# Two decode layers on one core: a query slice loaded ahead, output weights multiplied between the last values, smaller down pieces, fewer turning products

## The chip, the core and the metric

One core of a Trainium2 chip runs the whole program. Its engines are TensorE (PE, matrix products), VectorE (DVE), ScalarE (ACT), GpSimd (POOL) and SyncE (SP), whose queue issues nearly all transfers from HBM; 16 DMA engines carry them. The metric is the device time in microseconds (us), lower is better.

## The reference

One token for each of two sequences goes through attention and a gated feed-forward block, twice, with the same weights and the same caches:

```python
# B = 2, D = 576, H = 32 heads of 128, 8192 cached keys and values a head, Df = 4608, all float32
def attention(x):                       # x has been normalised
    q = (x @ wq) as heads
    p = softmax(q . k_cache / sqrt(128))
    return (p . v_cache) as one row @ wo
def feed_forward(x):
    return (gelu_tanh(x @ w_gate) * (x @ w_up)) @ w_down
x = x + attention(layernorm(x)); x = x + feed_forward(layernorm(x))     # layer one
x = x + attention(layernorm(x)); x = x + feed_forward(layernorm(x))     # layer two
```

## The kernel before

**Cache items.** Attention runs over items: 30 *pairs* (two heads of one sequence: 8.4 MB of keys and as much of values) and four *singles* (heads 30 and 31, s0 to s3, half as large). In layer one the singles come last, in the order s0, s1, s2, s3; layer two goes backward, so it begins with s3, s2, s1, s0. The keys and values of s3 and s2, the values of s1 and a quarter of its keys stay in the local memory between the layers and are not loaded again. For each part of an item, DVE multiplies the keys by the query (L490, `multiply`), POOL adds the halves (L494) and DVE reduces them (L500, `add_up`); then follow the maximum (`peak`, DVE L511, a transpose on PE L513, `highest`, DVE L518), the softmax on ACT (L529, L533), its total on PE (L546), the products with the values on PE (`values`, L561) and the joining of the result (`gather`, DVE L571 and L573; `context`, PE L581).

**The area and its queue.** All loads go into one tile, `space`. A class `Space` holds a list of loads in a fixed order; `pump` issues the first one when the place that it wants is clear, and none that stands behind it before. `done(key)` is called where the program has emitted the last use of a load; in the run, the transfer then waits for that use. Between the layers everything goes through a ring of 6,912 columns (`MID` to `END`): first the output weights `wo` of layer one (16 pieces of 1,152 columns, 576 KB: here w0 to w15), then gate and up weights (36 pieces), the down weights (12 pieces of 1,728 columns, 864 KB: d0 to d11), and the query weights of layer two (18 pieces of 1,024 columns, 512 KB: eight of one half, two of the middle rows, eight of the other half). The ring holds 3.5 MB. Scratch for s3 lies in the same ring until s3's scores are done, so only w0 and w1 can be loaded before that.

**Around the change.** In layer one, `values(s3)` is emitted first, then `invert`, `gather`, the products `project` with 14 of the 16 `wo` pieces, `context`, and the last two. In `mlp(0)`, `lower(d0)` stands ahead of `turned(1)` (72 small products that turn the second half of the hidden row, L693) and `gelu(1)`; the other down pieces follow (L715). In layer two, `attention` multiplies the whole first half of the query weights (L416), with `norm` after its first two pieces; ACT copies the queries (L440), `query(0)` (L462) spreads that of s3, and only then can DVE begin; `rest_of_queries` follows on PE behind `query(1)`. The loads behind the query weights are three parts of s1's keys (in the ring), s0's four parts of keys (where s3's keys lay), s0's values (where s3's values lay), and then the pairs: keys into the place of s2's keys and values, values into the place of s1, keys into the place of s0.

At the end, `mlp(1)` turns both halves (72 products each), and multiplies the down weights while their last pieces arrive.

The lines of the queue that the change touches:

```python
sp.at = MID + 2 * PART                                              # the ring's first place
first_down = [(t, lo, lo + 3) for t in range(NT) for lo in (0, 3, 6)]
```

Of the kernel before, what the change touches and what calls it, by code (L numbers as in the profile page):

```python
# [15 lines left out]
P = 128  # L16
# [23 lines left out]
NG = H // GH  # L40

# [54 lines left out]
def decode_layers(ctx, tc, x_in, kc, vc, wq, wo, wg, wu, wd, out):  # L96
# [52 lines left out]

    def middle(key, w, width, where, lo=0, hi=None):  # L150
# [48 lines left out]
    first_down = [(t, lo, lo + 3) for t in range(NT) for lo in (0, 3, 6)]  # L199
# [25 lines left out]
    sp.at = MID + 2 * PART  # L225
# [10 lines left out]
    for t, lo, hi in downs[0]:  # L236
        down(("d", 0, t, lo), mid, t, lo, hi)
    for half in (1, 0):
        for i in range(NW):
            for s in range(2):  # L240
                rows(("wq", 1, half, i, s), wq, HQ, mid, (2 * i + half) * HQ + s * CQ * 2, CQ * 2)
        if half:
            for s in range(2):
                middle(("wq", 1, "m", s), wq, HQ, mid, s * CQ * 2, (s + 1) * CQ * 2)
# [102 lines left out]
    def turn(first=False):  # L347
# [7 lines left out]
        if not first:  # L355
            nc.vector.tensor_copy(wide, x10[:, :, 0:9])
        nc.vector.tensor_copy(x10[:, :, 9:10], x10[:, :, 4:5])
        nc.vector.transpose(xtm, x10.rearrange("p q (r i) -> p i (q r)", i=5)[:, 4, :])
        nc.vector.tensor_mul(
            xm, xtm[:, 0:RW].unsqueeze(1).to_broadcast([P, 5, RW]), mask.unsqueeze(2).to_broadcast([P, 5, RW])  # L360
        )
# [3 lines left out]
        for b in range(B):  # L365
# [3 lines left out]
            )  # L369
        return apart  # L370
# [33 lines left out]
    def attention(layer, items, apart):  # L404
# [3 lines left out]
        def queries(bank, lhs, at, start, stop, s=None):  # L408
            for c in range(4):
# [3 lines left out]
                else:  # L413
                    moving = space[:, at + c * CQ // 2:at + (c + 1) * CQ // 2]
                    to = bank[32 * c:32 * c + WIN, s * CQ // 2:(s + 1) * CQ // 2]
# [13 lines left out]
        else:  # L429
            for i in range(NW):  # L430
                for s in range(2):
                    queries(acc[1], window(1, i), at_of["wq", 1, 1, i, s], i == s == 0, False, s)
                    done(("wq", 1, 1, i, s))
                if i == 0:
                    norm(apart)
            for s in range(2):
                queries(acc[1], only[1], at_of["wq", 1, "m", s], False, s == 1, s)
                queries(xps, only[0], at_of["wq", 1, "m", s], s == 0, False, s)
                done(("wq", 1, "m", s))
            nc.scalar.activation(qsb, acc[1], AF.Copy)  # L440
# [149 lines left out]
        def project(g):  # L590
            n = GH if layer else 2
            for i in range(GH):
# [211 lines left out]
```

## Time and profile before

| | |
|---|---|
| runs | 2707.04, 2707.79, 2709.14 us; median 2707.79 us |
| profiled execution | 2708.16 us, of which the span of its instructions is 2706.1 us and 2.1 us lie around it |
| busy share of the span | DMA queue q1 99.3% of 16 engines; DVE 69%, POOL 43%, PE 35%, ACT 3% |
| read from HBM | 1153.18 MB, 426 GB/s over the span |
| mean granted TensorE clock | 0.627 of full speed |

The page shows one execution in 40 slices with the DMA share and the GB/s of each. A view by windows gives the same for any stretch, with each engine's busy time; the timeline lists instructions with their start and length in us and, in brackets, how long the engine had been idle and what ended it. Records of a fp32 matrix product come in twos, so a piece of 8 products shows as x16.

### The profile page before, as it was taken

How to read it: one execution, taken by the hardware profiler on the slowest of the kernel's cores; microseconds unless marked ns; L12 is line 12 of the kernel's file. 1: busy time of each engine (PE TensorE's matmuls, PEld its weight loads, DVE VectorE, ACT ScalarE, POOL GpSimd, SP SyncE). 2: the span in 40 equal slices, each digit the busy share in tenths (PEclk: the TensorE clock that was granted, in tenths of full speed). 3: DMA queues.
4: the chain of work that ended last, by engine and by line, in shares of the span. 5: the costliest groups of instructions: out<-in, count | busy, mean ns of one | idle time of the engine just before them, and what ended most of it. 6: DMA issues, size and time to landing. Idle time of an engine off the chain costs nothing.

```text
span 2706.1 us, 20011 instructions
## 1 busy us (share of the span) xinstructions
PE 953.7 (35%) x8348; PEld 344.9 (13%) x8348; DVE 1869.9 (69%) x1330; ACT 93.1 (3%) x419; POOL 1171.7 (43%) x342
## 2 busy tenths in 40 slices
PE   1332333233223323335754332233223322332346
PEld 0110111011101111112121111011101110111123
DVE  4678767877787778777049767877787778777750
ACT  0000000000000000000000000000000000000000
POOL 2445444544454445444025444544454445445530
PEclk7656665666566656666666665666566656665677
DMA  9999999999999999999999999999999999999998
GB/s 419 434 434 431 431 433 433 434 434 434 434 434 433 432 431 432 432 429 383 405 364 416 431 434 433 432 434 432 434 432 431 432 434 432 434 434 433 434 424 368
DMA packets 35930, 1154.47 MB, mean 427 GB/s; under 512 B 4080, under 2 KB 4096, under 8 KB 14848
## 3 DMA queue, kind: packets, MB, share of 16 engines
q1 hardware_dynamic: 35816, 1153.19, 99.3%
q8 instruction: 65, 1.06, 0.2%
q14 instruction: 25, 0.20, 0.0%
q10 hardware_dynamic: 24, 0.01, 0.0%
HBM read 1153.18 MB, written 0.00 MB: 426 GB/s over the span
## 4 chain that ended last, share of the span: by engine, by line
DMA 22%; DVE 15%; PE 9%; POOL 7%; issue 1%; ACT 1%; POOLq 0%; DVEq 0%; ACTq 0%
DMA space<-in_A_k_cache_dram 17%; DVE space L490 8%; POOL space L494 7%; PE acc L561 6%; DVE S L500 5%; DMA space<-in_B_w_up_dram 2%; DMA space<-in_B_w_gate_dram 2%; DMA space<-in_B_w_down_dram 1%; DVE osb L573 1%; PE xps L715 1%; PE nb L521 1%; ACT prz L533 1%; DMA space<-in_A_wo_dram 1%; PE tot L543 0%; PE gu L693 0%
## 5 line engine op out<-in xcount | busy, mean ns | idle before, releaser
L494 POOL TENSOR_TENSOR space<-space 128x2048 f32<-128x2048 f32 (+1 forms) x332 | 1168.1, 3527 | 1304.3 <-DVE space L490 1159.8
L490 DVE TENSOR_TENSOR space<-space,qp 128x4096 f32<-128x4096 f32 (+1 forms) x332 | 1136.0, 3437 | 475.3 <-DMA space<-in_A_k_cache_dram 468.1
L500 DVE TENSOR_REDUCE S<-space 128x32 f32<-128x2048 f32 (+1 forms) x332 | 595.5, 1794 | 115.6 <-POOL space L494 112.7
L561 PE MATMUL acc<-space,prz 128*8 128x512 f32 x4096 | 592.7, 742 | 0.0
L581 PE MATMUL po<-weights,osb 128*32 128x1 f32 x1024 | 59.6, 201 | 1143.7 <-DVE osb L573 1143.7
L581 PEld LDWEIGHTS po<-weights,osb 128*32 128x32 f32 x1024 | 54.2, 154 | 1161.6 <-DVE osb L573 1161.4
L561 PEld LDWEIGHTS acc<-space,prz 128*8 128x8 f32 x4096 | 115.6, 103 | 414.6 <-issue 412.5
L513 PE MATMUL mT<-ident,m 128*1 128x128 f32 x68 | 25.0, 368 | 400.9 <-DVE m L511 400.9
L521 PE MATMUL nb<-m,strip 1*128 1x1 f32 x256 | 64.5, 350 | 36.2 <-DVE m L518 36.2
L573 DVE SCALAR_TENSOR_TENSOR osb<-acc,diag,osb 128x128 f32<-128x128 f32 x204 | 71.5, 351 | 7.2
L382 POOL TENSOR_TENSOR rstd<-ve,mhalf 128x2 f32<-128x2 f32 x4 | 2.8, 701 | 169.2 <-DVE ve L380 169.2
L586 ACT COPY oT<-po 64x4 f32<-64x4 f32 (+1 forms) x68 | 10.7, 157 | 1898.2 <-PE po L581 1898.2
L521 PEld LDWEIGHTS nb<-m,strip 1*128 1x128 f32 x256 | 58.7, 313 | 55.1 <-DVE m L518 55.1
L543 PE MATMUL tot<-rs,strip 128*128 128x2 f32 x120 | 35.0, 361 | 77.3 <-ACT prz L533 77.3
L513 PEld LDWEIGHTS mT<-ident,m 128*1 128x1 f32 x68 | 5.4, 79 | 413.1 <-DVE m L511 359.0
L533 ACT ACTIVATE prz<-S,nbs 64x128 f32<-64x128 f32 (+1 forms) x136 | 53.4, 392 | 3.3 <-ACT nbs L529 0.2
L543 PEld LDWEIGHTS tot<-rs,strip 128*128 128x128 f32 x120 | 29.8, 308 | 82.4 <-ACT prz L533 82.4
L673 PE MATMUL acc<-space,xt 128*6 128x288 f32 x256 | 29.0, 568 | 26.9 <-DMA space<-in_B_w_up_dram 14.6
L518 DVE TENSOR_REDUCE m<-mT 1x2 f32<-1x128 f32 (+1 forms) x68 | 18.9, 278 | 28.3 <-PE mT L513 28.3
L684 DVE COPY o<-acc 128x288 f32<-128x288 f32 x2 | 0.9, 457 | 50.6 <-PE acc L673 50.6
L715 PE MATMUL xps<-space,hT 128*2 128x144 f32 x576 | 29.2, 364 | 15.7 <-DMA space<-in_B_w_down_dram 10.5
L352 DVE TENSOR_TENSOR x<-xps,x 128x144 f32<-128x144 f32 x3 | 0.9, 308 | 48.8 <-PE xps L715 24.9
(89 smaller groups left out, 347.7 us busy)
## 6 DMA issues: line engine op xcount, KB each, us to landing
space<-in_A_k_cache_dram SPq DMA_DIRECT2D x6, 4096.0 KB, 17.9
space<-in_A_v_cache_dram SPq DMA_DIRECT2D x3, 4096.0 KB, 28.3
space<-in_B_w_down_dram SPq DMA_DIRECT2D x13, 864.0 KB, 7.2
space<-in_B_w_gate_dram SPq DMA_DIRECT2D x18, 576.0 KB, 7.6
space<-in_B_w_up_dram SPq DMA_DIRECT2D x18, 576.0 KB, 8.2
space<-in_A_wo_dram SPq DMA_DIRECT2D x16, 576.0 KB, 8.7
space<-in_A_wq_dram SPq DMA_DIRECT2D x18, 512.0 KB, 6.2
space<-in_A_wo_dram SPq DMA_DIRECT2D x8, 1152.0 KB, 30.7
```

Of the source, the lines that this page charges most:

```text
L490: nc.vector.tensor_tensor(out=u, in0=t, in1=qp[n % 2][:, 0:DH].unsqueeze(1).to_broadcast([P, j, DH]), op=ALU.mult)
L494: nc.gpsimd.tensor_tensor(out=half, in0=half, in1=u[:, :, DH // 2:], op=ALU.add)
L500: nc.vector.tensor_reduce(out=S[n][:, 16 * lo:16 * hi], in_=half, axis=AX.X, op=ALU.add)
L513: nc.tensor.transpose(peaks[n], m, ident)
L521: nc.tensor.matmul(low[n], one_of[e] if heads == 2 else ones[0:1, :], m1[:, e:e + 1], start=(e == 0), stop=(e == heads - 1),)
L533: nc.scalar.activation(prz[rows_, n % 2, 0:item.rows // 4, e, :], s[rows_, 0:item.rows].rearrange("p (g r) -> p g r", r=4), AF.Exp, bias=n ...
L543: nc.tensor.matmul(tot, ones, rs[:, n % 2, :], start=True, stop=True)
L561: nc.tensor.matmul(acc[n % 2][32 * c:32 * c + 8, :], prz[:, n % 2, g, :, :].rearrange("p e r -> p (e r)"), space[:, at:at + 4 * DH], start ...
L573: nc.vector.scalar_tensor_tensor(t, q[:, r, :], diag[:, r:r + 1], t, op0=ALU.mult, op1=ALU.add)
L581: nc.tensor.matmul(po[lo + 32 * e:lo + 32 * e + 32, n % 2, i:i + 1], t[:, i::GH], w[:, e:e + 1], start=True, stop=True,)
L673: nc.tensor.matmul(banks[half][s][32 * c:32 * c + WIN, 0:BF], lhs, space[:, lo:lo + BF], start=key not in done_first, stop=stop,)
L715: nc.tensor.matmul(xps[32 * c:32 * c + B, 0:CW], hT[t // 2][:, i, t % 2, :], space[:, a:a + CW], start=(t == 0 and i == 0), stop=(t == NT ...
```

## The change

Four things, and two changes of order.

1. *Layer one's output weights between the last values.* The ring now begins at `MID + 4 * 2 * D`, so that w0 to w5 fill it without overlap (before, w5 lay partly on w0). `values(s3)` takes eight of the pieces: after each quarter of its products it multiplies two of w0 to w7. The other pieces follow as before.
2. *Smaller down pieces* in layer one: 3, 2, 2, 2 rows of each ninth in place of 3, 3, 3, so 16 loads of 864 or 576 KB in place of 12.
3. *The last two heads' query columns ahead.* Right behind the down weights come four loads of 128 KB (256 columns of 1 KB rows) and one of 128 KB for the middle rows: the columns of heads 30 and 31. The first half's pieces lose them (five of them have 768 columns). PE multiplies these first, then `norm`; ACT copies that corner; `query(0)` and `query(1)` follow, and the rest of the first half (`first_of_queries`) and the other half come behind them on PE. In the load order, two parts of s0's keys now stand ahead of s1's three.
4. *36 turning products* in `mlp(1)` in place of 144: the hidden row is laid out so that 64 columns are turned at once.
5. Order: for an item behind a single, `highest`, `softmax`, `total` and `values` of that single are emitted ahead of the item's second `multiply`, not behind it; `turn` makes the statistics before the middle rows.

```diff
-    sp.at = MID + 2 * PART
+    sp.at = MID + 4 * 2 * D
-    first_down = [(t, lo, lo + 3) for t in range(NT) for lo in (0, 3, 6)]
+    first_down = [(t, lo, hi) for t in range(NT) for lo, hi in ((0, 3), (3, 5), (5, 7), (7, 9))]
+    def last_heads(key, where):
+        def load(a):
+            at_of[key] = a
+            for i in range(NW):
+                src = bass.AP(wq.tensor, wq.offset + (2 * i + 2) * HQ - TAIL, [[18 * HQ, HALF], [10 * HQ, 2], [1, TAIL]])
+                nc.sync.dma_start(space[:, a + i * TAIL:a + (i + 1) * TAIL], src)
+        sp.queue.append((key, where, NW * TAIL, load))
...
+    last_heads(("wq", 1, "t"), mid)
+    middle(("wq", 1, "tm"), wq, HQ, mid, HQ - TAIL, HQ)
     for half in (1, 0):
...
+                size = BODY if half == s == 1 else HQ // 2
...
+    for k in range(2):
+        cache("k", 1, s0, P1, k, k + 1)
     for k in range(1, 4):
         cache("k", 1, s1, home[("k",) + s1.name], k, k + 1)
-    for k in range(4):
+    for k in range(2, 4):
         cache("k", 1, s0, P1, k, k + 1)
...
         else:
+            at = at_of["wq", 1, "t"]
+            for i in range(NW):
+                queries(acc[0], window(1, i), at + i * TAIL, i == 0, False, 1, [3])
+            done(("wq", 1, "t"))
+            norm(apart)
+            queries(acc[0], only[1], at_of["wq", 1, "tm"], False, True, 1, [3])
+            queries(xps, only[0], at_of["wq", 1, "tm"], True, False, 1, [3])
+            done(("wq", 1, "tm"))
+            nc.scalar.activation(qsb[96:P, TAIL:], acc[0][96:P, TAIL:], AF.Copy)
+
+        def first_of_queries():
...
-        def values(n):
+        def values(n, between=()):
...
+                if g % 4 == 3:
+                    for piece in between[:2]:
+                        project(*piece)
+                    between = between[2:]
...
             for k, unit in enumerate(item.units):
+                if k == 1 and fresh:
+                    highest(n - 1)
+                    softmax(n - 1)
+                    total(n - 1)
+                    values(n - 1)
                 made = multiply(n, unit)
...
                         if layer == 1 and n == 0:
                             query(1)
+                            first_of_queries()
                             rest_of_queries()
...
-                values(n)
+                values(n, pieces[:8] if n == last and layer == 0 else ())
...
         def turned(half):
...
+            if layer:
+                t = t.rearrange("p s w -> p (s w)")
+                sel = spread.rearrange("p (c e g) b -> p e c g b", c=2, e=2)
+                for i in range(NI):
+                    for e in range(2):
+                        nc.tensor.matmul(
+                            gu[half][HALF * e:HALF * e + HALF, i, :, :, :], t[:, i::NI], sel[:, e, :, :, :],
+                            start=True, stop=True,
+                        )
+                return
```

More of the change, by code (lines that the diff above doesn't have):

```diff
@@ L406, in attention, with queries @@
         qsb = once.tile([P, CQ], F32, name="qsb", tag="row")
-        def queries(bank, lhs, at, start, stop, s=None):
-            for c in range(4):
+        def queries(bank, lhs, at, start, stop, s=None, cs=range(4)):
+            for c in cs:
                 if s is None:
@@ L601, in project @@
                     done(("wo", layer, g, i // n * n))
+        pieces = [(g, lo, lo + 2) for g in order[:-1] for lo in (0, 2)]
         query(0)
@@ L654, in attention @@
                 total(n)
-                values(n)
+                values(n, pieces[:8] if n == last and layer == 0 else ())
         invert(last)
         gather(last)
-        rest = order[3:] if layer else order
-        for g in rest[:-1]:
-            project(g)
+        for piece in pieces[8:] if layer == 0 else [(g,) for g in order[3:-1]]:
+            project(*piece)
         context(last)
-        project(rest[-1])
+        project(order[-1])
     def mlp(layer, apart):
@@ L671, in products @@
                 key = half, s, c
-                lo = at + c * BF
+                lo = at + (c * CF + s * BF if layer else c * BF)
                 nc.tensor.matmul(
@@ L748, in several @@
                     for s in range(2):
-                        products(u % 2, s, window(g, u // 2), at + s * CF * 2, u >= 6 and g == 1)
+                        products(u % 2, s, window(g, u // 2), at, u >= 6 and g == 1)
                 done((name, 1, off))
@@ L756, in mlp @@
                 for s in range(2):
-                    products(half, s, both, at_of["m", 1, half] + s * CF * 2, False)
+                    products(half, s, both, at_of["m", 1, half], False)
                 done(("m", 1, half))
```

58 lines of the change are left out of this document (34 added, 24 removed).

## The prediction

> **What bounds the kernel now.** I read the page's slices first, then windows over the stretches where the slices dip, then the timeline there.
>
> ```profile
> span 2706.1 us, 20011 instructions
> GB/s 419 434 434 431 431 433 433 434 434 434 434 434 433 432 431 432 432 429 383 405 364 416 431 434 433 432 434 432 434 432 431 432 434 432 434 434 433 434 424 368
> ```
> ```profile
> 100.00:1200.00 1100.00, 342.86 (x2564) 121.43 (x2564) 815.85 (x516) 36.81 (x169) 518.22 (x143) 0.61 1.00 432
> 1250.00:1300.00 50.00, 31.64 (x370) 12.88 (x366) 21.44 (x35) 2.56 (x13) 10.96 (x5) 0.70 0.90 361
> 1350.00:1400.00 50.00, 31.50 (x586) 14.24 (x586) 9.21 (x26) 1.18 (x3) 3.08 (x3) 0.74 0.97 364
> 1400.00:1450.00 50.00, 26.55 (x157) 9.43 (x153) 49.51 (x48) 3.45 (x17) 31.48 (x14) 0.57 0.97 403
> 1450.00:1500.00 50.00, 23.04 (x150) 7.25 (x142) 37.19 (x27) 2.35 (x11) 22.05 (x7) 0.71 0.98 410
> 1500.00:2600.00 1100.00, 346.66 (x2552) 121.35 (x2552) 816.72 (x513) 36.81 (x169) 519.00 (x142) 0.61 1.00 433
> ```
>
> The last columns are clock, DMA share and GB/s. The cache stages run at 432 to 433 GB/s with the DMA engines full: there bytes set the time, and nothing in the change alters their bytes or their loop, so 2,200 us stay. Time can only come from the stretch 1250 to 1500 and from the tail, and there only by moving the moment at which the last transfer lands. I count what each stage of that stretch loses against its own full rate, and how much of it the change fills. Measurement of this kernel can tell about 0.2% from no change, 5.4 us.
>
> **Output weights (gain 3.2).**
>
> ```profile
> 1270.00:1275.00 5.00, 4.58 (x24) 1.71 (x28) 0.33 (x2) 0.80 (x4) 0.00 (x0) 0.53 0.86 333
> 1275.00:1280.00 5.00, 5.00 (x92) 2.21 (x88) 1.40 (x4) 0.00 (x0) 0.00 (x0) 0.78 0.20 29
> 1280.00:1285.00 5.00, 1.73 (x44) 0.72 (x32) 0.00 (x0) 0.00 (x0) 0.00 (x0) 0.90 1.00 406
> ```
> ```profile
> 1271.40 6.46 PE L561 MATMUL acc<-space,prz 128*8 128x512 f32 x32
> 1277.68 2.62 PE L596 MATMUL xps<-space,oT 128*2 128x144 f32 x80
> 1278.17 1.96 SPq L184 DMA_DIRECT2D space<-in_A_wo_dram  x4
> 1282.02 0.67 PE L596 MATMUL xps<-space,oT 128*2 128x144 f32 x16 [1.71 <-DMA space<-in_A_wo_dram]
> 1284.25 1.14 PE L596 MATMUL xps<-space,oT 128*2 128x144 f32 x16 [1.56 <-DMA space<-in_A_wo_dram]
> 1285.68 1.14 PE L596 MATMUL xps<-space,oT 128*2 128x144 f32 x16 [0.29 <-DMA space<-in_A_wo_dram]
> ```
>
> Pieces land 1.43 us apart when the queue is full (1284.25 to 1285.68: 590 KB, 412 GB/s). w5 is issued only at 1278.17, when w0 has been multiplied after all of `values(s3)`, and is used at 1282.02. Against 412 the three windows lose 5 x (79 + 383 + 6) / 412 = 5.7 us. With the change w5 needs no wait and lands 1.43 behind w4. w0 and w1 are multiplied after the first quarter of the values: 1271.4 + 6.46/4 = 1273.0, then 0.52 (2.62/5) to 1.14 us a piece. So w6 is issued near 1273.9, w8 near 1277, w10 near 1280, w12 near 1284. From issue on an empty queue to use took 3.85 us here (1278.17 to 1282.02), so a transfer that is to follow its predecessor without a hole wants about 4 us between its own issue and the predecessor's landing. By that the even pieces have 3.3 to 4.4 us and lose some 0.5 each, 2.1 in all, on PE's mean between the two prices. PE's whole work there is 6.46 + 16 pieces at 0.52 to 1.14, ending at 1286 to 1296, still ahead of the gate weights. From the 5.7 go 2.1 and 0.4 for the new wait of DVE at `highest` behind s0:
>
> ```profile
> 1202.93 0.28 DVE L518 TENSOR_REDUCE m<-mT 1x2 f32<-1x128 f32 x1 [0.47 <-PE mT L513]
> ```
>
> That is what DVE waits where `highest` stands right behind `peak`. Behind s1 and s2 the `gather` of the item before lies between and covers it. All of DVE's further work on the singles queues behind that wait, and so does the end of s3. Gain 3.2; bounds 1.0 (PE at 1.14 throughout) and 5.3.
>
> **Down pieces (gain 2.7).**
>
> ```profile
> 1352.20 1.62 PE L715 MATMUL xps<-space,hT 128*2 128x144 f32 x24 [0.96 <-DMA space<-in_B_w_down_dram]
> 1372.98 0.92 PE L715 MATMUL xps<-space,hT 128*2 128x144 f32 x24 [0.49 <-DMA space<-in_B_w_down_dram]
> 1375.10 0.92 PE L715 MATMUL xps<-space,hT 128*2 128x144 f32 x24 [1.20 <-DMA space<-in_B_w_down_dram]
> 1378.70 0.92 PE L715 MATMUL xps<-space,hT 128*2 128x144 f32 x24 [2.68 <-DMA space<-in_B_w_down_dram]
> 1380.82 1.62 PE L715 MATMUL xps<-space,hT 128*2 128x144 f32 x24 [1.20 <-DMA space<-in_B_w_down_dram]
> ```
> ```profile
> 1367.84 0.33 SPq L175 DMA_DIRECT2D space<-in_B_w_down_dram  x1
> 1370.58 0.33 SPq L175 DMA_DIRECT2D space<-in_B_w_down_dram  x1
> ```
>
> d0 to d11 arrive between 1352.20 and 1380.82: 28.6 us for 11 steps that take 2.1 each when the queue is full, 23.1; lost 5.5. The SP rows are d9 and d10: d9 issued 5.1 us before d8 arrived (1372.98) lost nothing, d10 with 4.5 us before d9 lost 1.5. The cause is the ring: with pieces of 1,728, d3 must wait for d0's products, d4 for d1's behind the 72 turning products, and so on. With 3, 2, 2, 2, d2 wants only the last up piece and d3 the first middle piece, so both are issued before d0 has landed; behind them each place comes clear two rows at a time. Counting places and products through, d4 still comes short by about 1.1, d8 by 1.0, d6 by 0.4, with smaller holes 0.3: 2.8 of 5.5 remain. Bounds 0 and 5.
>
> **Query weights (loss 1.6).**
>
> ```profile
> 1388.33 0.62 PE L416 MATMUL acc<-space,xt 128*6 128x256 f32 x8 [0.63 <-DMA space<-in_A_wq_dram]
> 1389.60 0.62 PE L416 MATMUL acc<-space,xt 128*6 128x256 f32 x8 [0.66 <-DMA space<-in_A_wq_dram]
> 1395.24 4.49 DVE L490 TENSOR_TENSOR space<-space,qp 128x2048 f32<-128x2048 f32 x2 [7.20 <-PE qp L462]
> ```
>
> 512 KB land 1.27 us apart. The five small loads carry 640 KB: 1.6 us at that pace if bytes count, 6.4 us if a 128 KB transfer costs as much as a 512 KB one; no row shows rows of 1 KB. Packets of 4,608 and 4,096 bytes stand at 1.43 and 1.27 us for 8 a DMA engine, 179 and 159 ns: nearly in proportion, so I stay near the bytes: +0.3, up to +4.8. Second, PE now reaches the other pieces only behind `norm` and `query(0)`, some 4.5 us after the small loads, and the ring is by then full up to the seventh piece; the eighth comes 1.3 late. In all 1.6.
>
> The return: `query(0)` no longer stands behind ten pieces. From the end of the down stage, `turn` and four products (1.6), the chain of `norm` (3) and the query (0.6) bring DVE's first multiply to 5.4 us behind the last down product, instead of 12.8 (1382.4 to 1395.24). With the 2.7 above, DVE starts ten us sooner.
>
> **The start of layer two (gain 5.9).** In the windows 1400 to 1500 the rate falls short of 433 by 30 and 23 GB/s, 3.5 + 2.6 = 6.1 us.
>
> ```profile
> 1403.53 1.04 PE L416 MATMUL xps<-space,xt 128*6 128x256 f32 x8 [0.18 <-DMA space<-in_A_wq_dram]
> 1411.23 0.22 DVE L511 TENSOR_REDUCE m<-S 128x1 f32<-128x64 f32 x1
> 1453.25 0.33 SPq L136 DMA_DIRECT2D space<-in_A_v_cache_dram  x1
> 1473.34 0.33 SPq L136 DMA_DIRECT2D space<-in_A_k_cache_dram  x1
> 1496.48 4.42 DVE L490 TENSOR_TENSOR space<-space,qp 128x4096 f32<-128x4096 f32 x1 [10.68 <-DMA space<-in_A_k_cache_dram]
> ```
>
> After the last query piece (used 1403.53) nothing is queued, since s1's keys want the ring; later the pairs' values (1453.25) and keys (1473.34) are issued late, because DVE works without a break from 1395 on and frees their places last. With DVE ten us ahead, s0's first two key parts are issued before the query weights end and cover the first hole (0.2 left). Against it stands one new wait: PE is bound by `rest_of_queries` when DVE has done s3, 16 us after its start (1395.24 to 1411.23), so DVE stands still at `highest` for 2 to 4 us. The two late issues still come 8 us sooner, by then enough. Values of a single come 2.2 us sooner too. By 1496.48 DVE waits 10.68 us for a transfer: from there bytes rule again.
>
> **Tail (gain 0.5).**
>
> ```profile
> 2678.86 2.42 PE L693 MATMUL gu<-spread,o 128*32 128x4 f32 x144
> 2692.29 10.80 PE L715 MATMUL xps<-space,hT 128*2 128x144 f32 x265 [3.25 <-issue]
> 2695.00:2700.00 5.00, 5.00 (x136) 3.45 (x132) 0.00 (x0) 0.00 (x0) 0.00 (x0) 0.79 0.51 205
> 2700.00:2705.00 5.00, 3.09 (x97) 1.99 (x85) 0.31 (x1) 0.00 (x0) 0.00 (x0) 1.00 0.03 10
> ```
>
> Each half's turning costs 2.4 us, a quarter of that leaves 0.6: the down products could begin 3.6 us sooner. But the last transfer ends just behind 2700 (10 GB/s in the last window, 0.03 of the engines), and PE ends at 2703.1. So at most about a us comes of it; if the clock is granted at half then (x136 in 5 us against x97 in 3), PE could lose one. I take 0.5, from -1.5 to 1.
>
> **Weighed against the Trainium skill.** The row first: 590 KB pieces land 1.43 us apart. The Trainium skill, page "DMA: Bandwidth & Descriptors", section "Rules for kernel authors", asks for 1 MiB and more per transfer, and its "Bandwidth" section has 341 GB/s at 1 MB, 138 at 64 KB. By that the change goes the wrong way; by the row, 412 GB/s at 0.59 MB, it holds only where nothing is queued behind. The rule as a mechanism is the second rival.
>
> **Sum.** 3.2 + 2.7 - 1.6 + 5.9 + 0.5 = 10.7 us off the profiled execution's 2708.2: 2697.5. It stands 0.4 above the median of the runs shown, so 2697.0.
>
> **Rivals.** (1) *The holes are filled wholly*: every issue leads by 4 us or more. Then the down stage gives 5, the output weights 5.3, query weights lose 0.3, the rest as above: 16.4, 2691. For it: d9's row. Against: the short leads counted above.
> (2) *Each transfer pays in a ring*: what d0 to d11 lost is not a short lead but a price per transfer, 5.5/11 = 0.5 us. The stages then hold 16 + 23 transfers in place of 12 + 18, and the smaller ones, with less behind them, all pay: 39 x 0.5 = 19.5 against 5.5 now. DVE then starts only some 3 us sooner, so layer two's start gives 3: 3.2 - 14 + 3 + 0.5 = -7.3, 2715. It decides once most of the 39 lead by less than 4 us. Against it: the query pieces of 1388.33 and 1389.60 pay nothing.
> (3) *DVE's chain holds layer two back*: the small loads take 6.4 us and the wait behind `rest_of_queries` 5, so that DVE gains nothing there and the late issues stay: 3.2 + 2.7 - 6.4 + 3.5 + 0.5 = 3.5, 2704.
>
> **Chances.** Forecast and near it (gain 7 to 14) 0.58, rival 1 0.24, rival 3 0.10, rival 2 0.05, something in no row 0.03. Faster by over 0.2%: 0.58 + 0.24 and half of rival 3 and a little of the rest, 0.87; within 0.2%: 0.07; slower: 0.06. The range takes in rival 1 up to 17 us, and down to a gain of 4: 2690 to 2703.5.
>
> **What would show it.** Right: no 5 us window under 300 GB/s between 1265 and 1300; down products' arrivals 25 to 26 us from first to last; DVE's first multiply of layer two near 1382 instead of 1395; s0's keys issued before the last query piece lands; over 425 GB/s where 1400 to 1500 lay; PE waiting for the last down piece. Wrong: query pieces further apart than 1.3 us for most of the stage; DVE idle over 5 us behind s3; a hole before the pairs' values.

## The result, and the profile after

| | before | after | ratio, 95% interval |
|---|---|---|---|
| median of six runs each | 2708.52 us | 2698.91 us | 0.9965 (0.9952 to 0.9978) |
| profiled execution | 2708.16 us, span 2706.1 | 2698.30 us, span 2696.5 | |

The changed kernel is faster by 9.6 us (0.35%). The forecast was 2697.0, with 2690 to 2703.5. The total came out; three of its five terms did not.

The head and the slices of the page after, and windows of the changed kernel (the last three columns are granted clock, DMA share and GB/s):

```profile
span 2696.5 us, 19594 instructions
GB/s 420 434 434 433 435 428 435 434 431 435 432 429 435 431 435 435 432 428 411 410 365 435 432 435 434 433 433 430 434 434 432 434 435 431 432 430 435 433 426 375
```
```profile
1270.00:1275.00 5.00, 4.27 (x34) 2.38 (x38) 0.33 (x2) 1.05 (x5) 0.00 (x0) 0.50 0.97 369
1275.00:1280.00 5.00, 5.00 (x108) 2.61 (x100) 0.00 (x0) 0.00 (x0) 0.00 (x0) 0.91 0.97 358
1280.00:1285.00 5.00, 2.86 (x72) 1.33 (x64) 1.40 (x4) 0.00 (x0) 0.00 (x0) 1.00 1.01 378
...
1350.00:1400.00 50.00, 32.75 (x498) 13.52 (x494) 20.26 (x33) 1.26 (x4) 12.46 (x6) 0.75 0.94 347
1400.00:1450.00 50.00, 26.70 (x165) 9.61 (x161) 46.10 (x45) 3.45 (x17) 25.92 (x11) 0.69 1.03 436
1450.00:1500.00 50.00, 20.55 (x134) 7.32 (x134) 36.55 (x27) 2.50 (x12) 23.43 (x7) 0.64 0.99 429
```

The 29 GB/s of 1275 to 1280 have become 358, and 1400 to 1500 runs at 436 and 429 in place of 403 and 410. The stretch 1350 to 1400 has become slower, 347 in place of 364: there the loss still sits. PE's timeline over the output weights, the down weights and the query weights shows it:

```profile
1272.19 1.89 PE L601 MATMUL acc<-space,prz 128*8 128x512 f32 x8
1273.86 2.14 PE L640 MATMUL xps<-space,oT 128*2 128x144 f32 x32
...
1282.86 0.67 PE L640 MATMUL xps<-space,oT 128*2 128x144 f32 x16 [1.34 <-DMA space<-in_A_wo_dram]
...
1347.45 1.62 PE L771 MATMUL xps<-space,hT 128*2 128x144 f32 x24 [0.97 <-DMA space<-in_B_w_down_dram]
1348.85 2.39 PE L749 MATMUL gu<-spread,o 128*32 128x4 f32 x144
1351.08 2.10 PE L771 MATMUL xps<-space,hT 128*2 128x144 f32 x30
1355.14 3.88 PE L771 MATMUL xps<-space,hT 128*2 128x144 f32 x74 [1.97 <-issue]
1360.44 0.67 PE L771 MATMUL xps<-space,hT 128*2 128x144 f32 x16 [1.42 <-DMA space<-in_B_w_down_dram]
1364.01 1.11 PE L771 MATMUL xps<-space,hT 128*2 128x144 f32 x24 [2.90 <-DMA space<-in_B_w_down_dram]
...
1375.11 0.67 PE L771 MATMUL xps<-space,hT 128*2 128x144 f32 x16 [0.34 <-DMA space<-in_B_w_down_dram]
...
1381.97 5.40 PE L436 MATMUL acc<-space,xt 128*6 128x256 f32 x56
1390.80 0.62 PE L436 MATMUL acc<-space,xm 128*6 128x256 f32 x8 [3.43 <-DMA space<-in_A_wq_dram]
...
1402.06 1.02 PE L436 MATMUL xps<-space,xt 128*6 128x256 f32 x8 [0.62 <-DMA space<-in_A_wq_dram]
```

Two holes stand out: at 1355.14 PE stands 1.97 us on "issue", waiting for nothing that the profile names, in the middle of the products of the third piece; and at 1390.80 it waits 3.43 us for query weights. DVE and SP at the start of layer two:

```profile
1381.74 4.49 DVE L529 TENSOR_TENSOR space<-space,qp 128x2048 f32<-128x2048 f32 x2 [0.62 <-PE qp L501]
1403.41 0.28 DVE L557 TENSOR_REDUCE m<-mT 1x1 f32<-1x128 f32 x1 [5.46 <-PE mT L552]
1489.05 4.42 DVE L529 TENSOR_TENSOR space<-space,qp 128x4096 f32<-128x4096 f32 x1 [11.26 <-DMA space<-in_A_k_cache_dram]
```
```profile
1395.94 1.06 SPq L138 DMA_DIRECT2D space<-in_A_k_cache_dram  x2
```

DVE begins at 1381.74 in place of 1395.24. It meets the keys of the second pair, its first long wait for a transfer, at 1489.05 in place of 1496.48.

A table of stages makes all runs comparable. Each mark is a start in the timeline of the profiled execution: G the first gate product of layer one, D0 the first down product, D9 the product of the last down piece, Q the last query product, K the multiply of the second pair's keys (the last DVE row above). Columns are G itself, the lengths between the marks, and K to the end of the span; us. The ratio is to the kernel before as it ran beside each kernel, where its median lay between 2707.35 and 2708.52 us, so small differences are better read from the ratios than from the medians.

| kernel | G | G-D0 | D0-D9 | D9-Q | Q-K | K-end | median of the runs, ratio to before |
|---|---|---|---|---|---|---|---|
| before | 1299.57 | 52.63 | 28.62 | 22.71 | 92.95 | 1209.6 | 2708.52 |
| after | 1295.54 | 51.91 | 27.66 | 26.95 | 86.99 | 1207.5 | 2698.91, 0.9965 |
| after, again | 1297.06 | 52.04 | 27.62 | 27.33 | 86.85 | 1207.5 | 2698.68, 0.9966 |
| item 1 undone | 1298.58 | 53.59 | 28.20 | 27.29 | 86.96 | 1207.5 | 2702.02, 0.9980 |
| item 2 undone | 1296.29 | 52.18 | 26.87 | 27.90 | 86.96 | 1207.8 | 2699.85, 0.9971 |
| item 3 undone | 1296.07 | 52.66 | 27.69 | 25.04 | 92.51 | 1207.6 | 2701.35, 0.9978 |
| item 4 undone | 1296.31 | 53.66 | 27.58 | 26.00 | 86.70 | 1208.4 | 2700.69, 0.9978 |
| one order of item 5 undone | 1295.29 | 52.92 | 28.93 | 25.55 | 86.46 | 1207.5 | 2698.53, 0.9965 |
| first query pieces early | 1295.80 | 52.07 | 27.96 | 24.50 | 86.94 | 1207.4 | 2699.22, 0.9967 |
| turning cut in two | 1295.46 | 51.86 | 27.09 | 25.58 | 86.82 | 1207.5 | 2697.96, 0.9963 |
| both of these | 1295.52 | 52.25 | 26.27 | 24.05 | 86.07 | 1207.3 | 2696.69, 0.9960 |
| program shifted | 1296.04 | 57.85 | 26.34 | 25.60 | 86.56 | 1208.0 | 2703.81, 0.9984 |
| turning late | 1296.17 | 51.95 | 25.16 | 25.60 | 87.41 | 1207.4 | 2697.55, 0.9963 |
| turning late, first query pieces early | 1296.95 | 52.13 | 25.83 | 25.97 | 86.59 | 1207.4 | 2694.64, 0.9951 |

From before to after the differences are 4.0, 0.7, 1.0, -4.2, 6.0 and 2.2 us, 9.6 in all before rounding. Where the code of a stage is the same, its length scatters: G by 1.8 us over twelve profiles, D0-D9 by 1.3 over seven, D9-Q by 2.3 over nine, Q-K by 1.3, K-end by 0.7. So a single profile tells a change of the early stages only roughly. The time of one kernel has an interval of about 0.0025 of ratio, 7 us wide; single items of 1 to 3 us are read from the stages first. Part of the scatter goes with the granted clock: of the nine profiles of D9-Q, the three with a clock of 0.74 to 0.75 in that stage took 27.3 to 27.9 us, and the six with 0.83 to 0.89 took 25.6 to 27.0.

### The profile page after: what moved, and what is told of

The parts are those of the page before. It is cut to its first block, busy times and chain, and to the rows that moved or that the text cites. A ratio compares the mean times of both kernels' runs of the same rounds, so it can differ in the third digit from the quotient of the medians.

```text
span 2696.5 us, 19594 instructions
## 1 busy us (share of the span) xinstructions
PE 952.5 (35%) x8132; PEld 343.0 (13%) x8132; DVE 1870.6 (69%) x1330; ACT 93.5 (3%) x421; POOL 1171.5 (43%) x342
## 4 chain that ended last, share of the span: by engine, by line
DMA 20%; DVE 15%; PE 9%; POOL 7%; issue 4%; ACT 1%; POOLq 0%; DVEq 0%; SPq 0%
DMA space<-in_A_k_cache_dram 17%; DVE space L529 9%; POOL space L533 7%; PE acc L601 6%; DVE S L539 5%; DMA space<-in_B_w_down_dram 2%; DMA space<-in_B_w_up_dram 1%; DVE osb L617 1%; PE nb L560 1%; ACT prz L572 1%; DMA space<-in_A_wq_dram 1%; PE xps L640 0%; PE tot L582 0%; DMA space<-in_A_wo_dram 0%; PE mT L552 0%
## 5 line engine op out<-in xcount | busy, mean ns | idle before, releaser
L529 DVE TENSOR_TENSOR space<-space,qp 128x4096 f32<-128x4096 f32 (+1 forms) x332 | 1136.0, 3437 | 465.7 <-DMA space<-in_A_k_cache_dram 465.0
L552 PE MATMUL mT<-ident,m 128*1 128x128 f32 x68 | 25.2, 370 | 406.6 <-DVE m L550 406.6
L615 DVE TENSOR_SCALAR osb<-acc,diag 128x128 f32<-128x128 f32 x68 | 23.3, 342 | 19.1 <-PE acc L601 19.1
```

The costliest lines, as they stand in the source:

```text
L529: nc.vector.tensor_tensor(out=u, in0=t, in1=qp[n % 2][:, 0:DH].unsqueeze(1).to_broadcast([P, j, DH]), op=ALU.mult)
L552: nc.tensor.transpose(peaks[n], m, ident)
```

## The experiments

### Each item undone

**Item 1**, the output weights back behind the last values:

```diff
-                values(n, pieces[:8] if n == last and layer == 0 else ())
+                values(n)
-        for piece in pieces[8:] if layer == 0 else [(g,) for g in order[3:-1]]:
+        for piece in pieces if layer == 0 else [(g,) for g in order[3:-1]]:
```

> The changed kernel with item 1 alone undone: all 16 output-weight pieces are multiplied behind the last values again. Theory (the transfers bound, and what a stage loses stays lost): the last output-weight piece lands 3.5 to 4.0 us later against the span's start than in the changed kernel, where it landed at 1293.8, and the end moves by the same, so about 2702.7 us. Rival (the later stages win the time back, because each of them has slack of its own): under 1.5 us, so below 2700.5 us, with the piece still late by 3.5.

Measured: 2702.02 us, 3.2 over the mean of the two runs of the changed kernel. Its window shows the hole again:

```profile
1275.00:1280.00 5.00, 5.00 (x96) 2.20 (x92) 1.40 (x4) 0.00 (x0) 0.00 (x0) 0.86 0.43 128
```

128 GB/s in place of 358; not 29 as before, presumably since the ring's new first place lets w5 be issued early. G comes 1.5 to 3.3 us later than in the twelve profiles with item 1. What is lost there stays lost: no later stage makes up for it. The theory holds, a little under its size.

**Item 2**, 12 down pieces:

```diff
-    first_down = [(t, lo, hi) for t in range(NT) for lo, hi in ((0, 3), (3, 5), (5, 7), (7, 9))]
+    first_down = [(t, lo, lo + 3) for t in range(NT) for lo in (0, 3, 6)]
```

> The changed kernel with item 2 alone undone: the first layer's down weights come in 12 pieces of 3 blocks again in place of 16. Theory from comparing the traces (the smaller pieces were worth about 1 us and not the 2.7 of the prediction): about 2700 us, with the last down piece landing 1 us later against the last output-weight piece. Rival A (the prediction's 2.7): 2701.6 us. Rival B (a price for each of four more transfers, 0.5 us each, eats the gain): 2698 us or less.

Measured: 2699.85 us, 1.1 over the changed kernel, while its down stage took 26.87 us, 0.7 *less* than the shortest of the seven profiles that differ in the pieces alone there. The time's interval holds both. So rival A, the forecast's 2.7, is out by the stage, and a gain of the smaller pieces isn't shown. Nor is a loss: the down and the query stage together took 54.77, against 54.61 and 54.95 in the two profiles of the changed kernel. The Trainium skill, page "DMA: Bandwidth & Descriptors", section "Rules for kernel authors", asks for transfers of 1 MiB and more; the down stage alone agrees with its direction here, by 0.7 us, though not with a large price, as a later run shows.

**Item 3**, the query slice and the order of the keys undone (the code of before for layer two's query weights, and `cache("k", 1, s0, ...)` for four parts behind s1's three).

> The changed kernel with item 3 alone undone: no slice of the last two heads ahead, 18 query pieces of 512 KB, all four heads before the first value, and the keys of the first singles in the old order. Theory from comparing the traces: the query stage takes 4 us less than in the changed kernel and the start of layer two 6 us more, so slower by about 2 us, 2700.7 us; the key part that is the fourth of the first single then lands about 2 us later. Rival A (the prediction's terms, -1.6 and +5.9): slower by 4.3 us, 2703.2 us. Rival B (DVE's wait of 5.46 us behind the rest of the queries is on the path, and goes): faster by 2 us or more.

Measured: 2701.35 us, 2.5 over the changed kernel. DVE's first multiply of layer two and its multiply of the second pair's keys in this kernel (its L504 is the changed kernel's L529):

```profile
1393.01 4.49 DVE L504 TENSOR_TENSOR space<-space,qp 128x2048 f32<-128x2048 f32 x2 [9.83 <-PE qp L476]
...
1493.97 4.42 DVE L504 TENSOR_TENSOR space<-space,qp 128x4096 f32<-128x4096 f32 x1 [9.78 <-DMA space<-in_A_k_cache_dram]
```

DVE starts 11.3 us later and K lies 4.9 later. Q-K is 92.51, as long as before: item 3 is the gain of the start of layer two, 5.5 to 5.7 against the two profiles of the changed kernel (the slice and the order of the keys were undone together, so their shares aren't known). In the query stage it costs 0.5 to 2.9: 25.6 to 27.9 in the nine profiles with its order, against 25.04. Rival B is out. The theory's 4 us for the query stage were too much: 25.04 isn't the 22.71 of before, and about 2.3 us of that stage's loss came with the rest of the change. Undoing item 1 or item 2 alone did not bring them back either (27.29, 27.90). The granted clock is a candidate: over this stage it was 0.80 in the profile of before and 0.64 here, and the same 24 records (1385.75 there, 1380.88 here) took 1.95 and 2.61 us, so places of the ring may have come free later. That this makes up the 2.3 us isn't shown.

**Item 4**, 72 narrow products a half again in layer two (`turned` without its branch for layer two, and the columns laid out as before).

> The changed kernel with item 4 alone undone: layer two's gate and up products are turned by 72 narrow products for each half again. Theory (the tail gave what the turn saved): slower by 0.9 to 1.5 us at the end alone, about 2700.0 us; every row before the last gate and up piece unchanged. Rival (the tail's gain came from how the last transfers fell on the DMA engines): within 0.5 us of the changed kernel, and the time from the last landing to the end stays at 3.2 us.

Measured: 2700.69 us. The tails of PE, first of the changed kernel, then of this one:

```profile
2676.61 2.34 PE L740 MATMUL gu<-spread,o 128*64 128x8 f32 x36 [2.16 <-DVE o L730]
2678.88 6.16 PE L771 MATMUL xps<-space,hT 128*2 128x144 f32 x144
2686.99 2.39 PE L771 MATMUL xps<-space,hT 128*2 128x144 f32 x72 [1.94 <-DMA space<-in_B_w_down_dram]
...
2692.39 1.16 PE L771 MATMUL xps<-space,hT 128*2 128x144 f32 x32 [0.68 <-DMA space<-in_B_w_down_dram]
```
```profile
2677.95 1.84 PE L739 MATMUL gu<-spread,o 128*32 128x4 f32 x106 [1.78 <-issue]
...
2683.91 10.54 PE L761 MATMUL xps<-space,hT 128*2 128x144 f32 x256 [2.70 <-issue]
```

A group of 36 records takes 2.34 us where 144 took 2.4, so turning itself is no shorter. What goes is the standing on "issue", 1.78 and 2.70 us; without it PE waits for the last down pieces, and the transfers set the end. K-end is 0.9 us longer with 72 than in the changed kernel, 0.3 to 1.0 over all profiles with 36. The trace's packets say where: the last packet of data ends 4.8 us before the end of the span with item 4 undone, 3.9 in the changed kernel, 5.1 in the kernel before, and from K to that packet it is 1203.5 and 1203.6 us with and without the undoing. So the 0.9 lies behind the last landing. The theory holds at about 0.9; the time's 1.9 us more hold it within their interval.

**Item 5**, the order inside layer two (the other order, in `turn`, was not undone): the block `highest`, `softmax`, `total`, `values` of a single moved back behind the next item's second `multiply`.

> The changed kernel with one order of item 5 undone: a single's second statistics, totals and values stand behind the second multiply of the next item again. Theory (the start of layer two is bound by the transfers, and the order changes what DVE does early enough to keep the slots free): the release of the first pair's slot and with it the first pair's keys come later by what the second multiply takes, 2 to 4.5 us, and the time is 2 to 4 us over the changed kernel, about 2701.7 us. Rival (the slots are released early enough either way, and the gain of that stage is the key order's and the query slice's): within 1 us of the changed kernel, 2698 to 2700 us.

Measured: 2698.53 us, no change. The wait of 5.46 us at `highest` shrinks, since DVE multiplies once more ahead of it, and K stays:

```profile
1404.07 0.28 DVE L557 TENSOR_REDUCE m<-mT 1x1 f32<-1x128 f32 x1 [1.90 <-PE mT L552]
...
1489.15 4.42 DVE L529 TENSOR_TENSOR space<-space,qp 128x4096 f32<-128x4096 f32 x1 [12.85 <-DMA space<-in_A_k_cache_dram]
```

My theory was wrong, the rival right: 3.6 us more or less of DVE standing behind s3 change nothing at K, because DVE has 11 to 13 us to spare there.

**The changed kernel again**, as a measure of scatter:

> The changed kernel itself, once more, for its own scatter beside the others of this call. Expected: 0.9965 of the kernel before within 0.001, and every stage's landings within 1.5 us of the first profiled run.

Measured: 0.9966 (0.9954 to 0.9979), span 2698.4; G lay 1.5 us later, the other stages within 0.4.

### The stand at 1355

The same stand is in the profile of before (1.93 us at 1359.88). In all nine profiles in which the turning stands right behind the first down piece and nothing is added ahead of it, it comes after the same records: 24 + 144 + 30, the 198th product record from the first down product on. The page of the changed kernel has PE's records and its instruction packets:

```profile
PE 952.5 (35%) x8132; PEld 343.0 (13%) x8132; DVE 1870.6 (69%) x1330; ACT 93.5 (3%) x421; POOL 1171.5 (43%) x342
...
q8 instruction: 64, 1.05, 0.2%
```

8132 products and 8132 weight loads are 16,264 instructions, 254 for each of 64 packets of 16.4 KB; before there were 16,696 and 65 packets. So q8 seems to carry PE's own program, a packet for about 127 products. I cut the turning in two to see whether the narrow products or the packet make the stand:

```diff
             lower(*d[0])
-            turned(1)
+            turned(1, (0,))
+            lower(*d[1])
+            lower(*d[2])
+            turned(1, (1,))
             gelu(1)
-            for piece in d[1:]:
+            for piece in d[3:]:
```

> The changed kernel with layer one's second turning (72 x 2 products of 4 columns) cut in two: half of it behind the first down piece, the other half behind the third. Theory (behind 144 narrow products in a row PE stands 2 us for want of instructions, and that delays the release of the third down piece and with it the issue of later ones): the stand of about 2 us at 1355 falls under 1 us, the down stage takes 1 to 2.5 us less than the 27.7 of the changed kernel, and the time falls by as much. Rival A (the stand is paid by each row of narrow products, so it comes twice, about 1 us each): the down stage is unchanged within 0.7 us. Rival B (the down stage is set by the distance between the ring's end and its reader, not by this stand): the stand goes, the last down piece lands where it landed.

```profile
1351.22 1.25 PE L750 MATMUL gu<-spread,o 128*32 128x4 f32 x70
1355.60 0.23 PE L750 MATMUL gu<-spread,o 128*32 128x4 f32 x1 [3.13 <-issue]
```
```profile
q8 instruction: 1, 0.02, 3.0%
```

The first fence is PE's timeline. The stand neither shrank nor came twice: it took 3.13 us, at the upper end of the 1.3 to 3.1 of the nine, and fell between the 70th record of the second part and its last two, which is 24 + 72 + 32 + 70 = 198 again. The second is the queue view over 1352.5 to 1354.5: one q8 packet moved there, while PE stood. So the place in the program decides, and all three readings that I had put down were wrong about the stand.

The traces' packet records tie the stand to that packet more closely. In all eleven profiles that have the stand (these nine, the cut turning, and the run with both moves below), PE goes on 1.2 to 1.6 us after the end of one q8 packet, whether it stood 1.3 or 3.1 us: in the changed kernel the packet ends at 1353.61 and PE goes on at 1355.14. That packet had begun when PE was at most 10 records short of the place where it stood. PE's stands on "issue" in the tail, of the kernel before and of the one with item 4 undone, end 1.3 to 1.6 us after such a packet too, and in the tail of item 4 undone the second comes 106 + 3 + 1 + 18 = 128 records behind the first. Four profiles have a shorter one as well, 0.3 to 0.6 us in layer one's first turning, 383 records ahead of the stand or of its place; these end 1.3 to 1.5 us after a packet.

The down stage is 0.5 us under the shortest of its peers, and the time 0.7 under the changed kernel, within its scatter.

**The program shifted.** If the packet's edge is the cause, moving the edge into the middle of the narrow products must remove the stand:

```diff
                             done(key)
+                            if half == g == 1:
+                                for _ in range(13):
+                                    nc.tensor.matmul(gu[0][0:32, 0, 0, :, :], o[0][:, 0, 0::NI], sel0, start=True, stop=True)
```

(`sel0` stands for the first quarter of `spread`.)

> The changed kernel with 104 useless narrow products added to PE in layer one's gate and up stage, 13 behind each of the last eight up pieces, where PE waits 0.3 to 0.8 us for each piece; nothing else is moved. The stand of about 2 us at 1355 fell behind the same 198th product from the first down piece in the changed kernel and with the turning cut in two, and the queue named instruction moved one packet just ahead of its end. Theory (the stand is PE's wait for the next packet of its own program; the packet is asked for about 128 products ahead, and 144 narrow ones use them up in less time than it takes): with 104 products more the packet's edge lies in the middle of the 144, the narrow ones fall half on each side, the stand falls under 0.7 us, and the last down piece lands 0.5 to 2 us earlier although PE has more to do. Rival (narrow products in a row cost the stand, wherever the packet's edge is): the stand stays at 1.3 to 2 us behind the 198th product, and the down stage at 27.7.

```profile
1348.01 1.69 PE L787 MATMUL gu<-spread,o 128*32 128x4 f32 x25
...
1355.28 2.41 PE L749 MATMUL gu<-spread,o 128*32 128x4 f32 x144
1357.48 1.69 PE L771 MATMUL xps<-space,hT 128*2 128x144 f32 x48
```

The stand is gone: the 144 run in 2.41 us and 48 records follow without a pause, past the 198th. So the narrow products in a row are not the cause by themselves. The rest of the expectation failed. The 104 products are 208 records and moved the edge twice as far as I had said (to about 10 records ahead of the first down product, and about the 117th behind it). And 25 of them took 1.69 us, 68 ns a record where the turning takes 17; why is not shown. PE fell behind the up pieces and G-D0 grew by 6 us: 2703.81 us, about 5 over the changed kernel. The down stage itself, 26.34, is 1.2 under the shortest of its peers, but begins with pieces waiting, so that it proves little.

**Turning late.** The same test without more work: the first eight down pieces use the first half alone, so the turning can stand behind the seventh, and the edge falls at its 70th record.

```diff
-            lower(*d[0])
+            for piece in d[:7]:
+                lower(*piece)
             turned(1)
             gelu(1)
-            for piece in d[1:]:
+            for piece in d[7:]:
```

> The changed kernel with layer one's second turning and its gelu behind the seventh down piece in place of the first (the first eight down pieces use the first half alone). Theory (the packet's edge, 198 products behind the first down piece's start, then lies 70 products into the 144): no stand over 0.7 us, the third to seventh pieces are released as they land, the down stage falls from 27.7 to 25.5 to 26.5 us, and the time by 1 to 2 us. Rival A (narrow products in a row): the stand of 2 us comes behind them, at the eighth piece, and the stage gains under 0.5 us. Rival B (the ninth piece waits for DVE's gelu, 1.6 us behind the turning): the stage gains nothing and the wait of PE named there is DVE's.

```profile
1358.99 2.35 PE L749 MATMUL gu<-spread,o 128*32 128x4 f32 x144
1361.20 0.66 PE L771 MATMUL xps<-space,hT 128*2 128x144 f32 x16
1363.08 5.28 PE L771 MATMUL xps<-space,hT 128*2 128x144 f32 x72 [1.23 <-DVE hT L764]
```

No stand: the q8 packet had begun 110 records ahead of the place and ended at 1356.60, and PE passed the place at 1360.02. The new wait for DVE's gelu (rival B) is 1.23 us and costs less than the stand did. The down stage is 25.16 us, 2.4 under the shortest of its peers, and 25.83 in the run below: just the "25 to 26" that the prediction had named for the smaller pieces. But this edit does two things: it takes away the stand, and it moves the turning itself, 2.4 us, behind the products that free the first places. SP's issue of the eighth piece, which follows the third piece's products, shows both, first in the changed kernel and then here:

```profile
1355.81 0.33 SPq L189 DMA_DIRECT2D space<-in_B_w_down_dram  x1
```
```profile
1352.08 0.33 SPq L189 DMA_DIRECT2D space<-in_B_w_down_dram  x1
```

That is 8.4 us behind the first down product in the changed kernel and 4.0 here. Of the 4.4 us between them the stand is about 2.0 and the turning 2.4. With the turning in place and no stand there is only the shifted program (26.34). So how much of the stage's 2.4 us is the stand's is not shown.

With pieces of 0.59 to 0.88 MB, 9.7 MB behind the first piece in 25.2 us are 387 GB/s. The Trainium skill, page "DMA: Bandwidth & Descriptors", section "Bandwidth", has 341 GB/s for transfers of 1 MB, issued from GpSimd; the run is above that with smaller ones, issued by SP and queued behind each other. The time, 2697.55 us, has the ratio 0.9963 against 0.9965: right in sign, within the scatter.

### The hole at 1390

**First query pieces early.** The eighth query piece and the first of the middle rows need the places of the first two pieces, which PE multiplied only behind the first half's scores, at 1381.97.

```diff
+        if layer:
+            first_of_queries(0, 1)
         query(0)
...
-                            first_of_queries()
+                            first_of_queries(1, NW)
```

> The changed kernel with one step moved: the two query pieces of the first block pair of x are multiplied ahead of the first half's scores of the queries, behind the slice of the last two heads, and not behind them. Theory (the query stage of the changed kernel holds a hole of 3.4 us because the eighth query piece and the first piece of the middle rows can only be issued when those two pieces have been multiplied, and PE does that only at 1382): the hole at 1387 to 1391 goes, the last query piece lands 2 to 3.5 us earlier, and the end moves by as much, to about 2696 us. Rival (PE is busy or waiting on DVE's vectors at 1379 to 1382 anyway, so the first half's scores only start later by what the two pieces take, and DVE's chain with them): the query stage gains under 1 us and DVE's first chain starts 0.7 to 1.5 us later; time within 1 us of the changed kernel.

```profile
1389.08 1.04 PE L436 MATMUL acc<-space,xm 128*6 128x256 f32 x8 [1.64 <-DMA space<-in_A_wq_dram]
```
```profile
1382.46 4.49 DVE L531 TENSOR_TENSOR space<-space,qp 128x2048 f32<-128x2048 f32 x2 [0.62 <-PE qp L503]
```

The wait ahead of the middle rows is 1.64 in place of 3.43 us. DVE starts 6.63 us behind the last down product, as in the changed kernel (1381.74 behind 1375.11), so the two pieces fit into PE's wait for DVE's vectors and the rival's price is not paid. The stage is 24.50 us against 25.6 to 27.9 in nine profiles with the changed order. The time, 2699.22, shows no gain beside the 2698.68 of the changed kernel on the same chip: by time this stays inconclusive.

**Both** the cut turning and the early pieces:

> The changed kernel with both moves: the first two query pieces ahead of the first half's scores, and the second turning cut in two. Theory: the two gains add, 3 to 5 us under the changed kernel, about 2694.5 us. Rival (one hole filled only moves the next one, because both stages are held by the same ring): not more than the larger of the two alone.

Measured: 2696.69 us, 2.0 under the changed kernel, with the two stages at 26.27 and 24.05: by the medians more than either alone and less than the theory's sum, but the intervals (0.9946 to 0.9974 against 0.9954 to 0.9979) overlap.

**Turning late, first query pieces early:**

> The changed kernel with both moves that emptied a wait: layer one's second turning behind the seventh down piece, and layer two's first two query pieces ahead of the first half's scores. Theory (each wait delays releases in the same ring, and both are gone): no stand of PE on its own program in the down stage, which takes 25 to 26 us; query stage 24 to 25 us; the last query piece lands at 1397 to 1399, 4 to 5 us earlier than in the changed kernel, and the time is 3 to 4 us under its 2698.8, about 2695.3 us. Rival (the later start of layer two's pairs absorbs what is won ahead of it): at most 1 us under the changed kernel, with the first pairs' keys landing where they did.

Measured: 2694.64 us, ratio 0.9951 (0.9937 to 0.9964), against 0.9965 (0.9952 to 0.9978) of the changed kernel: the lowest of all medians, 13.4 us under the 2708.02 of the kernel before on its chip. By the ratios that is 3.8 us under the changed kernel, near the theory's 3 to 4, but the intervals still overlap. In its windows the stretch that was left behind runs faster, 374 GB/s in place of 347:

```profile
1350.00:1400.00 50.00, 34.94 (x582) 14.56 (x574) 20.25 (x33) 1.26 (x4) 11.44 (x6) 0.73 0.99 374
```

The down stage went as expected, 25.83, without the stand. The query stage, 25.97, did not: a wait of 1.89 us ahead of the middle rows is still there, and its last query product starts at 1400.88 and not by 1399. The profiled execution of this kernel, 2696.72, is the slowest of its five, so its stages show less than the median does.

## Why the prediction came out

Five of the six signs that the prediction named for being right came: no window of 5 us under 300 GB/s between 1265 and 1300 (the lowest is 358), DVE's start, the keys of s0, the rate of 1400 to 1500, and PE's wait for the last down piece. The arrivals of the down pieces, 27.66 us and not 25 to 26, failed.

**What bounds it: right up to the tail.** The cache stages still run at their rate, and the gains between 1250 and 1500 were transfers that landed sooner. In the tail 1.2 of the 2.2 us lie behind the last landing (5.1 to 3.9 us), so there PE's own work set the end of the kernel before.

**Output weights, 3.2 forecast: right.** 4.0 and 2.5 in the two profiles, 3.2 by undoing it in time. Windows of 358 to 378 GB/s, not 412, fit the short leads of the even pieces that it had counted.

**Down pieces, 2.7 forecast: wrong.** 1.0 measured, and with larger pieces the stage was no longer but shorter (26.87). The step that failed is "counting places and products through": it let d1 and d2 run behind the turning at their own price, and did not read the stand of 1.93 us on "issue" that the timeline of before had there. That stand held back the release of the third piece, so that the eighth was issued at 1355.81 only; PE then waited 1.42 us for it and 2.90 for the ninth. With neither the stand nor the turning ahead of the second piece the stage takes 25.2 to 25.8 us, within 25 to 26; the share of each is not shown. Whether 12 pieces would do as well with the turning late wasn't tried.

**Query weights, -1.6 forecast: mis-sized,** -4.2 and -4.6 by the stage. Item 3 itself costs 0.5 to 2.9, which holds the 1.6; "the eighth comes 1.3 late" left out the first piece of the middle rows, which waits for the same products, and early products of the first pieces take part of it back. About 2.3 us more came with the rest of the change or with a lower granted clock, and stay unexplained. The small loads were not the loss: in the profile after, PE waited for none of the five.

**Start of layer two, 5.9 forecast: right.** 6.0, and 5.5 to 5.7 go with item 3 undone. DVE begins at 1381.74 (1382 forecast) and the keys of s0 are issued at 1395.94, ahead of the last query product. The wait behind `rest_of_queries` is 5.46 us and not 2 to 4. DVE idle for over 5 us behind s3 had been named as a sign against the forecast; it came, and cost nothing, because the transfers were queued ahead of it.

**Tail, 0.5 forecast: wrong.** 2.2 by K-end, above its bound of 1, and item 4 is 0.9 of it. The step that failed is "a quarter of that leaves 0.6": 36 records take as long as 144 did, and what went were PE's stands on "issue". Of the other 1.3 us, 1.0 is a shorter way from K to the last landing (1204.6 to 1203.6), which no item undone brings back; its cause is open.

**The rivals.** The price for each transfer (2715) is out: 387 GB/s with pieces of 0.59 to 0.88 MB. DVE's chain (2704) is out: 11.26 us to spare at K. The filled holes (2691) came nearest in the last run, 2694.64, after two edits which the change does not hold. That the sum was right is in part luck: it missed 1.7 us in the down pieces and 2.6 in the query weights, and against these stood 1.7 in the tail, 0.8 in the output weights and 0.7 of G-D0, for which it had no term.

## What to carry to other kernels

A step that is all small instructions can run an engine out of its own program: look in the timeline for idle time on "issue", count the instructions from a fixed point in two kernels, look in the queue view for an instruction packet that ends just ahead of the restart, and move the step to where the engine waits for data anyway. In a ring of loads, a late product delays the load that takes its place, here the eighth piece behind the third; a place that frees the next loads wants to be multiplied before work that nobody waits for. Price a wait by who waits next: 5.5 us of an idle engine cost nothing where 11 us of slack lay behind it.

## What the runs showed of the hardware

PE's program seems to come over the DMA engines while it runs: 64 packets of 16.4 KB on q8 for 16,264 instructions, 254 each. Where 96 to 98 of the 128 records ahead of that packet's place were narrow ones of 17 ns each, PE stood 1.3 to 3.1 us, in all eleven profiles at the same place of its program, and went on 1.2 to 1.6 us after the packet's end. In the three in which the packet had begun over 100 records ahead of that place, it did not stand. The Trainium skill, page "DMA: Bandwidth & Descriptors", section "Queues, rings and completion order", puts refills on row 14, which it calls runtime-internal, of the queue rows that all use the same 16 DMA engines; here the packets that go with PE's count and with its stands are those of q8. That the packet's lateness comes from the data queued on the same engines was not tried.
